# The moving operand of the big matmuls read as pairs of columns 256 apart

## The chip, the cores and the metric

The kernel runs on one core of one Trainium2 chip. A core has a matrix engine (TensorE, PE in the profile; its weight loads stand apart as PEld), VectorE (DVE), ScalarE (ACT), GpSimd (POOL) and SyncE (SP), which here issues nearly all DMA transfers. The metric is device time in microseconds, the median of several runs; work of the host before and after is not in it.

## The reference, cut to what matters

Attention over pooled keys and values, then a two-layer network with the activation h · erf(softplus(h)). All results are float32.

```python
k_p = k.reshape(B, H, S // 8, 8, D).mean(axis=3)      # B 8, H 8, S 576, D 64; v_p alike
attn = softmax(q @ k_p.T / sqrt(D))                   # 72 pooled keys
x = (attn @ v_p).transpose(0, 2, 1, 3).reshape(4608, 512)
h = x @ w_in                                          # 512 -> 2048
g = h * erf(log(1 + exp(h)))
out = g @ w_out                                       # 2048 -> 512
```

## The kernel before

**Layout.** Everything after the attention is kept transposed: features on the 128 partitions, tokens along the free dimension. The 4,608 tokens are cut into nine chunks of 512 (`TC`, `NC`). The stationary operand of a big matmul is a 128 x 128 block of a weight matrix, the moving operand a tile of 128 features by 512 tokens, and the result 128 features by 512 tokens in one bank of PSUM. A column of every moving tile, every bank and every output tile is thus one token.

**Three passes a product.** To come near float32, each operand is split into a high and a low part of type float32r (`halves`: a rounding copy on ScalarE or GpSimd, a subtraction on VectorE or GpSimd), and the helper `three` (line 817) issues three matmuls into the same bank: high x high, high x low, low x high. All big matmuls are on its line 821, as are the products of the later attention blocks with the split values (`att<-e,va` and `att<-e,vr` in the profile).

**Stages.** Chunk 0 runs plainly: `plain_in` computes its h, four feature tiles at a time, with the weights as they arrive and are split; `second` multiplies the activated tiles by w_out. The weights' parts are written to HBM tensors and read again later in pieces of 256 KB (`piece`). Chunks 1 to 8 run as four pairs s = 1 to 4. For each pair `quad` computes h by a scheme of seven products in place of eight (Strassen-Winograd: sums of weight blocks times differences of token tiles; `sides` makes the token tiles, `sums` the weight blocks). One call of the inner `product` (line 866) is six passes; a pair has 8 x 7 of them, 336 passes. The results are combined by VectorE (`t<-t,h`, `g<-t,h`), the activation runs on ScalarE (table loads, Softplus, Erf) and the multiplication by h on GpSimd or VectorE. The second layer of pair 1 goes through `second`; that of pairs 2 to 4 through `seconds`, again with seven products of 48 passes, whose moving operands are differences of g tiles (line 980), split anew. The last product of pair 4 goes through `rows`, output block by output block, its last pass cut into halves of 256 columns so that the end can be stored in pieces. The attention of the next tokens (`job`: scores in plain float32, transposes, values) is woven in between.

**What sets the order.** The program first lists operations, each with an engine, a cost in ns, a due time and the tiles that it reads and writes. `Program.once` (line 260) plays them as a list schedule over PE, ACT, DVE, POOL and SP: on each engine the operation that could start first, weighed against its due time, and within a window of due times; buffers and banks come from counted pools, and some operations may go to either of two engines. A DMA of 256 KB costs 720 ns on SP in this play, a float32r pass of 512 columns 227 ns on PE. `Program.order` (line 227) plays eight times; after each play it works out how late every operation could have ended (`latest`), and these times are the due times of the next. It keeps the due times that came out of the shortest play, shifts some of them, and emits the order of one more play. The shifts come from the tuple `MOVES`: each number in it seeds random offsets (of 300, 1,000 or 3,000 ns in spread) to the due times of all operations within 6, 20 or 60 us of one point. Each engine then executes its list in this order; waits are made from the tiles' uses. Fillers (small bf16 matmuls, line 1115) are put into PE's list where the play has it idle at the start.

The lines that matter for the change:

```python
at = list(best[1])                                   # due times left by the shortest play
for seed in MOVES:
    ...                                              # shifts part of `at`
for prios in ([t / UNIT for t in at], best[2]):
    ...
    return self.once()                               # the order that is emitted
```

Of the kernel before, what the change touches and what calls it, by code (L numbers as in the profile page):

```python
# [22 lines left out]
NP = H // 2  # L23
NT = B * S
DM, DF = 512, 2048
P = 128
TC = 512
NC = NT // TC
NJ = DF // P

# [10 lines left out]
BY_BLOCK = lambda ck: True  # L41
PASSES, UNIT = 8, 5100.0
SPREAD, REACH, SPAN = (300.0, 1000.0, 3000.0), (6e3, 20e3, 60e3), 860e3
MOVES = (
# [5 lines left out]
T0, T0_STEP = -10.5, 1.5  # L50
VAL_R = 3.5
KEYS, KEYS_R, KEYS_S = -5.5, 0.5, -1.0
# [37 lines left out]
def blocks():  # L90


    out, qo = [], 0
    for b in range(B):
        t = 0
        while t < S:
            ck, off = divmod(b * S + t, TC)
            n, tiles, fresh = min(256 if b < SPLIT else TC, S - t, TC - off), [], t == 0
            for at in range(0, n, P):
                T = min(P, n - at)  # L100
                tiles.append((qo, T))
                qo += P * NP * T
            out.append((ck, b, tiles, off, fresh))
            t += n
    return out


def mix(x):
# [273 lines left out]
def moe_attention(ctx: ExitStack, tc: tile.TileContext, cst, qa, kl, vl, wi, wo, out):  # L382
# [16 lines left out]
    op = pr.op  # L399
# [155 lines left out]
    xt, made, values_of = {}, {}, {}  # L555
# [261 lines left out]
    def three(o, w, x, first, last):  # L817

        (wh, wl), (xh, xl) = w, x
        for q, (u, v) in enumerate(((wh, xh), (wh, xl), (wl, xh))):  # L820
            nc.tensor.matmul(o, u, v, start=first and q == 0, stop=last and q == 2, skip_group_check=True)  # L821

    def activation(hs, prio):

        ys = [Buf(space, [P, 2, 512], F32, "d", "d") for _ in range(2)]
        y = lambda k: ys[k // 2].ap[:, k % 2]
        own = [(ys[k // 2], k % 2) for k in range(4)]

        for i in (0, 2):

            def softplus(i=i):
                for k in (i, i + 1):
                    nc.scalar.activation(y(k), hs[k][0].ap, AF.Softplus)  # L833

            op("ACT", 2 * act(512), prio + 0.01 * i, softplus, [h for h, _ in hs[i:i + 2]], own[i:i + 2], funcs="softplus")
        for k in range(2):
            op("ACT", act(1024), prio + 0.2, lambda k=k: nc.scalar.activation(ys[k].ap, ys[k].ap, AF.Erf),  # L837
               own[2 * k:2 * k + 2], own[2 * k:2 * k + 2], funcs="sigmoid")
        for k, (h, g) in enumerate(hs):
            if g is h:  # L840
                both(True, dve(512), gps(512), prio + 0.3, lambda e, k=k, h=h: e.tensor_mul(  # L841
                    h.ap, y(k), h.ap), [own[k], h], [h])
            else:
                op("DVE", dve(512), prio + 0.3, lambda k=k, h=h, g=g: nc.vector.tensor_mul(
                    g.ap, y(k), h.ap), [own[k], h], [g])

    def plain_in(ks, base):

        hs = []
        for k in ks:  # L850
            ft = order[k]
            hi, lo = load_in(ft, base + 0.5 * k)
            ph = bank("h")

            def gemm(ph=ph, hi=hi, lo=lo):
                for p in range(NP):
                    sl = slice(P * p, P * p + P)
                    three(ph.ap, (hi.ap[:, sl], lo.ap[:, sl]), [x.ap for x in xt[0][p]], p == 0, p == NP - 1)

            op("PE", 12 * 227, base + 0.5 * k, gemm, [hi, lo, *(x for q in xt[0] for x in q)], [ph])  # L860
            g = place("g")
            gs[0, ft] = g
            hs.append((ph, g))
        activation(hs, base + 0.5 * ks[-1] + 1)

    def product(o, w, name, x, prio, more, last):

        xs = [t for k in range(2) for t in x[name, k]]
        ws = [w] if isinstance(w, Buf) else w[:2]
        half = lambda l: w.ap[:, l] if isinstance(w, Buf) else w[l].ap[:, w[2]]  # L870

        def go():
            for k in range(2):
                sl = slice(P * k, P * k + P)
                three(o.ap, (half(0)[:, sl], half(1)[:, sl]), [t.ap for t in x[name, k]],
                      not more and k == 0, last and k == 1)

        op("PE", 6 * 227, prio, go, [*ws, *xs], [o], turn="p")

    def head(s, i, x, due):  # L880

# [68 lines left out]
    def second(ck, k, due, ws, part):  # L950

        g = gs[ck, order[k]]
        gh, gl = place("gl", F32R), place("gl", F32R)
        halves(lambda: g.ap, lambda: gh.ap, lambda: gl.ap, due - 1, [g], gh, gl, turn="g")
        if k == 0:
            po[ck] = [bank("o") for _ in range(NP)]
        for j0 in (0, 2):

            def gemm(j0=j0, o=po[ck]):
                for j in (j0, j0 + 1):  # L960
                    three(o[j].ap, [part(ws, j, l) for l in range(2)], (gh.ap, gl.ap), k == 0, k == NJ - 1)

            op("PE", 6 * 227, due + 0.12 * j0, gemm, [gh, gl, *ws], [po[ck][j0], po[ck][j0 + 1]])
        if k == NJ - 1:
            for j in range(NP):
                o, ot = po[ck][j], place("f")
                out_of_bank(512, due + 0.3, lambda ot=ot: ot.ap, lambda o=o: o.ap, [o], [ot])
                store(ck, j, ot, due + 0.4)

    def seconds(s, base, span):  # L970

        a, b = 2 * s - 1, 2 * s
# [9 lines left out]
        def product(n, weights, moving, combine, onto=None, last=True):  # L982
            o = onto or [bank("o") for _ in range(2)]
            for i in range(NQ):
                due = base + step * (n + i / NQ)
                if combine:
                    u, v = combine
                    less(moving[i], u[i], v[i], due - 1.2)
                g = moving[i]
                gh, gl = place("gl", F32R), place("gl", F32R)  # L990
                halves(lambda g=g: g.ap, lambda gh=gh: gh.ap, lambda gl=gl: gl.ap, due - 1, [g], gh, gl, turn="g")
                w = piece(*weights(i), due)

                def gemm(gh=gh, gl=gl, w=w, i=i):
                    for j in range(2):
                        sl = slice(P * j, P * j + P)
                        three(o[j].ap, (w.ap[:, 0, sl], w.ap[:, 1, sl]), (gh.ap, gl.ap),
                              onto is None and i == 0, last and i == NQ - 1)

                op("PE", 6 * 227, due, gemm, [gh, gl, w], o, turn="p")  # L1000
            return o, base + step * (n + 1)

        def add(dst, u, v, prio):
# [11 lines left out]
        def rows(n, weights, moving, add_to):  # L1015
            o = [bank("o") for _ in range(2)]
            ws, gs_ = [], []
            for i in range(NQ):
                due = base + step * (n + i / NQ / 2)
# [5 lines left out]
            for j in range(2):  # L1025
                for i in range(NQ):
                    due = base + step * (n + (i / NQ + j) / 2)
                    (gh, gl), w = gs_[i], ws[i]
                    end = i == NQ - 1
                    for u, m in ((0, 256), (256, 256)) if end and j else ((0, 512),):  # L1030
                        def gemm(j=j, i=i, gh=gh, gl=gl, w=w, cs=slice(u, u + m), end=end):
                            sl = slice(P * j, P * j + P)
                            three(o[j].ap[:, cs], (w.ap[:, 0, sl], w.ap[:, 1, sl]), (gh.ap[:, cs], gl.ap[:, cs]), i == 0, end)

                        op("PE", 3 * (m / 2.4 + 14), due, gemm, [gh, gl, w], [(o[j], u)] if m < 512 else [o[j]], turn="p")
                ot = place("f")
                for u, m in ((0, 256), (256, 256)) if j else ((0, 512),):
                    cs, key = slice(u, u + m), u if j else None
                    op("DVE", dve(m), due + 0.2, lambda ot=ot, j=j, cs=cs: nc.vector.tensor_add(  # L1039
                        ot.ap[:, cs], add_to[j].ap[:, cs], o[j].ap[:, cs]), [add_to[j], (o[j], key)], [(ot, key)])  # L1040
                    op("SP", 720 * m / 512, due + 0.3, lambda ot=ot, j=j, cs=cs: nc.sync.dma_start(
                        out[b, j][:, cs], ot.ap[:, cs]), [(ot, key)], [])
# [28 lines left out]
    gs, po = {}, {}  # L1071
# [89 lines left out]
```

## Time and profile before

| | us |
|---|---|
| median of 3 runs (lowest, highest) | 844.68 (844.62, 845.06) |
| span of the profiled execution | 844.4 |
| TensorE busy in it | 833.6 |
| VectorE, ScalarE, GpSimd busy | 676.7, 572.6, 448.2 |

The page of the profile gives the span, from the first to the last instruction, for the execution that was profiled; the other times come from runs without a profile. Busy time counts a stretch once even where two matmuls overlap in it. A TensorE instruction's mean duration includes the time until its result has landed, which the next instruction overlaps: for the pitch of a dense stretch its length is divided by the number of instructions. An idle time is put down to the engine or transfer whose signal came last.

### The profile page before, as it was taken

To read this page: it belongs to the slowest core of one execution; us is meant where nothing else is said; L and a number is where in the kernel's file an instruction comes from. 1 tells how busy PE (TensorE), PEld (TensorE's weight loads), DVE (VectorE), ACT (ScalarE), POOL (GpSimd) and SP (SyncE) were. 2 spreads that over 40 slices of the span, in tenths; PEclk is the share of its full clock that TensorE was granted. 3 is DMA by queue.
4 is the path that set the end of the run, shared out by engine and by line. 5 is a ranking of instruction groups with operands and counts; after the bars stand their busy time and mean duration, and the time that the engine had idled before them with its cause. 6 is when DMAs were issued, how large, how long until landed. Compare 5 with 4: busy or idle time off the path is not lost.

```text
span 844.4 us, 13334 instructions
## 1 busy us (share of the span) xinstructions
PE 833.6 (99%) x4042; PEld 692.6 (82%) x4042; DVE 676.7 (80%) x1238; ACT 572.6 (68%) x979; POOL 448.2 (53%) x437
## 2 busy tenths in 40 slices
PE   7999999999999999999999999999999999999998
PEld 6788888777888888888888888888888888888886
DVE  5977887857888897798998978878889866668872
ACT  5999976589965561779785643888857517776630
POOL 2996893676978740375774342657444503442310
PEclk9999999999999999999999999999999999999999
DMA  9999999999999799975575677934655778347641
GB/s 331 316 332 344 373 361 377 328 355 322 355 318 366 257 369 358 360 244 151 156 239 178 190 261 240 339 124 124 197 182 160 256 233 306 129 145 254 183 159 54
DMA packets 134695, 218.03 MB, mean 258 GB/s; under 512 B 17120, under 2 KB 49248, under 8 KB 134624
## 3 DMA queue, kind: packets, MB, share of 16 engines
q1 hardware_dynamic: 134624, 217.18, 75.3%
q8 instruction: 33, 0.54, 0.3%
q14 instruction: 38, 0.31, 0.1%
HBM read 167.84 MB, written 49.28 MB: 257 GB/s over the span
## 4 chain that ended last, share of the span: by engine, by line
PE 75%; DVE 1%; ACT 0%; DVEq 0%; issue 0%
PE o L821 37%; PE h L821 30%; PE att L632 3%; PE att L821 2%; PE att L687 1%; PE att L751 1%; PE att L690 0%; DVE g L841 0%; DVE gl L441 0%; PE att L750 0%; DVE e L703 0%; ACT e L701 0%; DVE f L1039 0%; DVEq L1157 0%
## 5 line engine op out<-in xcount | busy, mean ns | idle before, releaser
L821 PE MATMUL o<-gl,w 128*128 128x512 f32 x1536 | 359.3, 392 | 0.1
L821 PEld LDWEIGHTS o<-gl,w 128*128 128x128 f32 x1536 | 285.9, 188 | 60.0 <-DVE gl L441 0.5
L821 PE MATMUL h<-x,w 128*128 128x512 f32 x1344 | 312.6, 391 | 0.9 <-DVE t L917 0.7
L821 PEld LDWEIGHTS h<-x,w 128*128 128x128 f32 x1344 | 250.8, 188 | 54.4 <-DVE t L917 1.7
L841 POOL TENSOR_TENSOR g<-d,g 128x512 f32<-128x512 f32 x83 | 108.9, 1332 | 116.4 <-ACT d L837 116.4
L441 POOL TENSOR_TENSOR gl<-g,gl 128x512 fp32r<-128x512 f32 x64 | 98.7, 1551 | 77.7 <-ACT gl L429 64.9
L429 ACT ACTIVATE gl<-g 128x512 fp32r<-128x512 f32 x175 | 104.0, 625 | 45.4 <-PE o L821 20.4
L441 DVE TENSOR_TENSOR gl<-g,gl 128x512 fp32r<-128x512 f32 x144 | 103.4, 744 | 4.6 <-ACT gl L429 4.2
L917 DVE TENSOR_TENSOR g<-t,h 128x512 f32<-128x512 f32 x96 | 65.5, 684 | 28.0 <-PE h L821 26.0
L833 ACT ACT_TABLE_LOAD x49 | 62.9, 1283 | 20.7 <-PE h L821 20.0
L837 ACT ACTIVATE d<-d 128x1024 f32<-128x1024 f32 x72 | 74.1, 1056 | 0.5
L833 ACT ACTIVATE d<-g 128x512 f32<-128x512 f32 x103 | 59.6, 624 | 6.1 <-DVE g L917 5.6
L980 POOL TENSOR_TENSOR g<-g 128x512 f32<-128x512 f32 x34 | 47.2, 1387 | 27.5 <-DVE g L980 15.3
L917 DVE TENSOR_TENSOR t<-t,h 128x512 f32<-128x512 f32 x57 | 39.1, 686 | 22.6 <-PE h L821 19.8
L837 ACT ACT_TABLE_LOAD x44 | 56.5, 1283 | 0.8
L429 ACT ACTIVATE x<-xr 128x512 fp32r<-128x512 f32 (+2 forms) x53 | 28.9, 562 | 36.1 <-DVE xr L795 23.1
L632 PE MATMUL att<-kbd,q 128*128 128x144 f32 (+1 forms) x320 | 46.9, 288 | 0.1
L821 PE MATMUL h<-x,ws 128*128 128x512 f32 x192 | 46.0, 391 | 0.7 <-DVE g L917 0.7
L632 PEld LDWEIGHTS att<-kbd,q 128*128 128x128 f32 (+1 forms) x320 | 41.8, 179 | 4.4 <-issue 1.9
L980 DVE TENSOR_TENSOR g<-g 128x512 f32<-128x512 f32 x62 | 44.2, 721 | 0.7
L821 PEld LDWEIGHTS h<-x,ws 128*128 128x128 f32 x192 | 35.8, 188 | 8.8 <-DVE g L917 1.4
L641 DVE TENSOR_REDUCE m<-att 128x4 f32<-128x288 f32 (+1 forms) x80 | 34.5, 447 | 9.6 <-PE att L632 9.1
(105 smaller groups left out, 1089.5 us busy)
## 6 DMA issues: line engine op xcount, KB each, us to landing
w<-ws SPq DMA_DIRECT2D x192, 256.0 KB, 4.4
w<-wo SPq DMA_DIRECT2D x136, 256.0 KB, 4.2
w<-wi SPq DMA_DIRECT2D x96, 256.0 KB, 5.1
ws<-ws SPq DMA_DIRECT2D x64, 256.0 KB, 5.1
v<-vl SPq DMA_DIRECT2D x48, 256.0 KB, 5.1
out<-f SPq DMA_DIRECT2D x35, 256.0 KB, 2.1
k<-kl SPq DMA_DIRECT2D x32, 256.0 KB, 5.2
q<-qa SPq DMA_DIRECT2D x32, 256.0 KB, 5.1
```

The source lines that it names most:

```text
L429: op("ACT", act(n), prio, lambda: nc.scalar.activation(dst(), src(), AF.Copy, scale=scale), *access, turn=turn, alt=("POOL", 0.833 * n + 1 ...
L441: both(True, dve(n), gps(n), prio + 0.1, lambda e: e.tensor_sub(lo(), src(), f32(hi())), reads + [hikey], [lokey])
L632: nc.tensor.matmul(o, raw.ap[:, p, :T], kbd[:, p], start=(p % 2 == 0), stop=True, skip_group_check=True)
L641: op("DVE", dve(4 * SP), r + 0.4, lambda pv=pv, gs=gs: nc.vector.tensor_reduce(m.ap[:T, gs], pv(), AX.X, ALU.max), [ps], [(m, g)])
L687: nc.tensor.transpose(pa.ap[:, P * p:P * p + T], sp[:, p, 0:P], ident[:T, :T])
L751: nc.tensor.matmul(o[0:64], vb[0:96, p], etb.ap[0:96, p // 2, :n], start=False, stop=True, skip_group_check=True)
L821: nc.tensor.matmul(o, u, v, start=first and q == 0, stop=last and q == 2, skip_group_check=True)
L833: nc.scalar.activation(y(k), hs[k][0].ap, AF.Softplus)
L837: op("ACT", act(1024), prio + 0.2, lambda k=k: nc.scalar.activation(ys[k].ap, ys[k].ap, AF.Erf), own[2 * k:2 * k + 2], own[2 * k:2 * k + 2 ...
L841: both(True, dve(512), gps(512), prio + 0.3, lambda e, k=k, h=h: e.tensor_mul(h.ap, y(k), h.ap), [own[k], h], [h])
L917: op("DVE", dve(512), prio, lambda: nc.vector.tensor_add(dst.ap, u.ap, o.ap), [u, o], [dst])
L980: both(True, dve(512), gps(512), prio, lambda e: e.tensor_sub(out.ap, u.ap, v.ap), [u, v], [out])
```

## The change

A new helper `pairs` stands in place of `three` at the five places that issue big matmuls (`plain_in`, both `product`, `second`, `rows`). The moving tile is viewed as two halves of 256 columns, and the columns are read alternately from the two: 0, 256, 1, 257, and so on. The result is written into the bank in address order. So after each of the two layers the tokens of a chunk stand in another order; the order after both is `TOKEN`, and the host undoes it on the output. The products of the attention go on through `three`.

In the plan, the cost of a pass of 512 columns goes from 227 to 216.3 ns (`PASS`), that of a half pass of 256 columns from m / 2.4 + 14 to m / 2.4 + 3. The tuple `MOVES` is emptied.

```diff
+PASS = 216.3
...
-MOVES = (
-    31000001, 31000009, 31000022, 31000054, 31000055, 31000061, 31000085, 31000111, 31000112, 31000135, 31000169,
...
+MOVES = ()
...
+def pair_order(n):
+
+    j = np.arange(n)
+    return n // 2 * (j % 2) + j // 2
+
+
+TOKEN = pair_order(TC)[pair_order(TC)]
...
+    def pairs(o, w, x, first, last, cs=slice(0, TC)):
+
+
+        at = slice(cs.start // 2, cs.stop // 2)
+        three(o[:, cs].rearrange("p (a b) -> p a b", b=2), w,
+              [t.rearrange("p (b a) -> p a b", b=2)[:, at] for t in x], first, last)
...
-                    three(ph.ap, (hi.ap[:, sl], lo.ap[:, sl]), [x.ap for x in xt[0][p]], p == 0, p == NP - 1)
+                    pairs(ph.ap, (hi.ap[:, sl], lo.ap[:, sl]), [x.ap for x in xt[0][p]], p == 0, p == NP - 1)
-            op("PE", 12 * 227, base + 0.5 * k, gemm, [hi, lo, *(x for q in xt[0] for x in q)], [ph])
+            op("PE", 12 * PASS, base + 0.5 * k, gemm, [hi, lo, *(x for q in xt[0] for x in q)], [ph])
...
-                            three(o[j].ap[:, cs], (w.ap[:, 0, sl], w.ap[:, 1, sl]), (gh.ap[:, cs], gl.ap[:, cs]), i == 0, end)
+                            pairs(o[j].ap, (w.ap[:, 0, sl], w.ap[:, 1, sl]), (gh.ap, gl.ap), i == 0, end, cs)
-                        op("PE", 3 * (m / 2.4 + 14), due, gemm, [gh, gl, w], [(o[j], u)] if m < 512 else [o[j]], turn="p")
+                        op("PE", 3 * (m / 2.4 + 3), due, gemm, [gh, gl, w], [(o[j], u)] if m < 512 else [o[j]], turn="p")
...
-    return r.results[0]["out"].transpose(0, 3, 1, 2).reshape(NT, DM)
+    return r.results[0]["out"][..., np.argsort(TOKEN)].transpose(0, 3, 1, 2).reshape(NT, DM)
```

The other three places change in the same way as `plain_in`.

## Rows read from the trace of the kernel before

**Rows 1.** The page: span, busy time of the engines, TensorE's clock in 40 slices.

```profile
span 844.4 us, 13334 instructions
PE 833.6 (99%) x4042; PEld 692.6 (82%) x4042; DVE 676.7 (80%) x1238; ACT 572.6 (68%) x979; POOL 448.2 (53%) x437
PEclk9999999999999999999999999999999999999999
```

**Rows 2.** TensorE's waits, to 120 us, then after: us in total, times, longest.

```profile
PE att L1115 <- DMA cst<-cst: 2.7, 1, 2.7
PE att L690 <- POOL bb L675: 1.8, 2, 1.6
...
PE h L821 <- DVE g L917: 0.7, 1, 0.7
PE h L821 <- DVE t L917: 0.7, 1, 0.7
```

**Rows 3.** The chain that ended last: start us, length us, what.

```profile
688.46 76.16 PE h L821 x336
764.62 76.20 PE o L821 x339
```

**Rows 4.** Groups of the big passes: busy us, mean ns; then idle before.

```profile
L821 PE MATMUL o<-gl,w 128*128 128x512 f32 x1536 | 359.3, 392 | 0.1
L821 PE MATMUL h<-x,w 128*128 128x512 f32 x1344 | 312.6, 391 | 0.9 <-DVE t L917 0.7
L821 PEld LDWEIGHTS o<-gl,w 128*128 128x128 f32 x1536 | 285.9, 188 | 60.0 <-DVE gl L441 0.5 <-POOL w L441 0.4 <-issue 0.2
L821 PE MATMUL h<-x,ws 128*128 128x512 f32 x192 | 46.0, 391 | 0.7 <-DVE g L917 0.7
L821 PE MATMUL o<-gz,w 128*128 128x512 f32 x45 | 10.4, 389 | 0.0
```

**Rows 5.** Other matmuls: a chain piece, a group, three lines of the timeline.

```profile
240.77 1.96 PE att L632 x16
L1115 PE MATMUL att<-cst 128*128 128x256 bf16 x131 | 18.9, 300 | 2.7 <-DMA cst<-cst 2.7
23.54 1.58 PE L1115 MATMUL att<-cst 128*128 128x256 bf16 x13
294.33 0.40 PE L821 MATMUL att<-e,va 128*128 128x256 f32 x2
295.75 0.40 PE L821 MATMUL att<-e,va 128*128 128x256 f32 x2
```

**Rows 6.** Busy us by stretch, clock, DMA share, GB/s; last, L821 alone.

```profile
40.00:120.00 80.00, 79.89 (x391) 65.97 (x390) 66.22 (x120) 75.25 (x115) 67.43 (x77) 1.00 1.00 352
120.00:360.00 240.00, 238.37 (x1163) 199.14 (x1162) 195.12 (x369) 156.81 (x268) 145.75 (x146) 1.00 0.98 343
360.00:620.00 260.00, 259.91 (x1275) 216.85 (x1274) 225.01 (x432) 190.84 (x311) 149.87 (x138) 1.00 0.61 201
220.00:240.00 20.00, 20.00 (x95) 16.41 (x94) 17.03 (x32) 18.57 (x25) 18.12 (x17) 1.00 1.04 384
40.00:120.00 80.00, 68.68 (x294) 54.28 (x293) 1.00 1.00 352
120.00:360.00 240.00, 215.02 (x930) 171.25 (x929) 1.00 0.98 343
```

**Rows 7.** ScalarE and GpSimd: stepped and plain reads of 512 elements, mean ns.

```profile
L490 ACT ACTIVATE cv<-d 128x512 f32<-128x512 f32 x32 | 19.7, 625 | 2.0 <-DVE etb L719 1.1 <-ACT cv L490 0.4 <-DVE s L657 0.3
L429 ACT ACTIVATE gl<-g 128x512 fp32r<-128x512 f32 x175 | 104.0, 625 | 45.4 <-PE o L821 20.4 <-DVE g L980 17.5 <-DVE g L844 4.6
L496 POOL TENSOR_SCALAR low<-d 128x512 uint32<-128x512 uint8 x21 | 16.8, 798 | 20.7 <-DMA d<-wi 13.9 <-DMA d<-wo 5.6
L430 POOL TENSOR_SCALAR gl<-g 128x512 fp32r<-128x512 f32 x33 | 23.2, 706 | 18.6 <-PE h L821 7.4 <-PE o L821 7.3 <-DVE g L844 2.1
```

More of the change, by code (lines that the diff above doesn't have):

```diff
@@ L874, in go @@
                 sl = slice(P * k, P * k + P)
-                three(o.ap, (half(0)[:, sl], half(1)[:, sl]), [t.ap for t in x[name, k]],
+                pairs(o.ap, (half(0)[:, sl], half(1)[:, sl]), [t.ap for t in x[name, k]],
                       not more and k == 0, last and k == 1)
-        op("PE", 6 * 227, prio, go, [*ws, *xs], [o], turn="p")
+        op("PE", 6 * PASS, prio, go, [*ws, *xs], [o], turn="p")
     def head(s, i, x, due):
@@ L960, in gemm @@
                 for j in (j0, j0 + 1):
-                    three(o[j].ap, [part(ws, j, l) for l in range(2)], (gh.ap, gl.ap), k == 0, k == NJ - 1)
-            op("PE", 6 * 227, due + 0.12 * j0, gemm, [gh, gl, *ws], [po[ck][j0], po[ck][j0 + 1]])
+                    pairs(o[j].ap, [part(ws, j, l) for l in range(2)], (gh.ap, gl.ap), k == 0, k == NJ - 1)
+            op("PE", 6 * PASS, due + 0.12 * j0, gemm, [gh, gl, *ws], [po[ck][j0], po[ck][j0 + 1]])
         if k == NJ - 1:
@@ L996, in gemm @@
                         sl = slice(P * j, P * j + P)
-                        three(o[j].ap, (w.ap[:, 0, sl], w.ap[:, 1, sl]), (gh.ap, gl.ap),
+                        pairs(o[j].ap, (w.ap[:, 0, sl], w.ap[:, 1, sl]), (gh.ap, gl.ap),
                               onto is None and i == 0, last and i == NQ - 1)
-                op("PE", 6 * 227, due, gemm, [gh, gl, w], o, turn="p")
+                op("PE", 6 * PASS, due, gemm, [gh, gl, w], o, turn="p")
             return o, base + step * (n + 1)
```

4 rows, old and new, of the table MOVES are left out of this document.

## The prediction, made before the result was known

> **What bounds the kernel now.** The summary comes first: TensorE is busy 833.6 of 844.4 us, no other engine over 80%, and its clock is granted in full in every slice [rows 1]. As a busy TensorE is not one at its peak, the second view is who TensorE waits for. Hardly for anyone: the first constants, short waits while the attention starts up, and after 120 us two waits of 0.7 us each [rows 2]. The third view, the chain that ended last, is TensorE on TensorE for the last 152 us: 336 passes of 512 columns in 76.16 us, and 339 in 76.20, six of them half as wide [rows 3]. So the end is set by how many passes there are and by the time from one start to the next. That time is 76.16 / 336 = 226.7 ns. The mean of some 390 ns that the profile gives one pass [rows 4] holds its latency, which the next pass overlaps; the pitch is what counts.
>
> 512 columns at 2.4 GHz take 213.3 ns, so each pass pays 13.4 ns beyond its columns. Other forms pay less. The plain fp32 score matmuls run 16 records in 1.96 us, 122.5 ns each: for 144 columns that is twice 60.0 ns, and 2.5 over. The bf16 fillers take (1.58 - 0.30) / 12 = 106.7 ns for 256 columns, nothing over, with the group's mean of 300 ns taken for the last one's latency [rows 5]. The score matmuls take two cycles a column and the fillers read half as many bytes a column; only the float32r passes read four bytes at every cycle, and they do it in address order. So the 13.4 ns belong to this form, not to TensorE's issue as such, and the read pattern is the one part of the form that the change touches.
>
> **The change, part by part.**
>
> *The passes.* Full-width passes in the loops that the change touches: 1,536 + 1,344 + 192, and in the last product 45 and six halves, worth 48 [rows 4]: 3,120. (The 120 attention passes that go through the same helper keep their order.) Neither their number nor their weight loads change, and their output is written in address order as before. What one costs afterwards no row shows. From below: its columns alone, 213.3 ns, which takes 13.4 x 3,120 = 41.8 us off. From above: no row has TensorE with an alternating read, so the nearest are the other engines' stepped reads. ScalarE's read of one 4-byte word in eight bytes takes 625 ns, like its plain copy at 625; GpSimd's of one byte in eight takes 798 against 706 [rows 7], 13% more, by which a pass would take 256 ns and the kernel 3,120 x 29.5 = 92 us more. I take 213.3 + 2.5 = 215.8 ns, from the nearest row on the same engine with a four-byte operand: 10.9 x 3,120 = 34.0 us less. The weight loads, 188 ns at the mean [rows 4], still fit under that pitch.
>
> The Trainium skill (TensorE: Matmul & The Clock Gate, "Wait — 56ns, not 53.3ns?") gives a back-to-back matmul N / 2.4 GHz plus about 2.5 ns, 215.7 ns at 512 columns. The score matmuls here agree with it and the 226.7 ns of the big passes don't; with the page's figure the gain would be 11.0 x 3,120 = 34.3 us.
>
> *What is late next.* With 34 us less in TensorE, the stretches where something else is as full lose part of it. From 40 to 120 us the DMA engines are full (share 1.00, 352 GB/s) and ScalarE is busy 75.25 of 80; from 120 to 360 us the DMA share is 0.98 at 343 GB/s [rows 6]. At most 294 and 930 passes lie there, so TensorE would give 3.2 and 10.1 us, and the same bytes would have to come at 352 x 80 / 76.8 = 367 and 343 x 240 / 229.9 = 358 GB/s. If the present rates are the ceiling, all 13.3 us are lost; if the 384 GB/s of the best 20 us [rows 6] can be held, nothing. The wanted rates lie 47% and 37% of the way up, so I charge 1.5 + 3.7 = 5.2 us. After 360 us the DMA share is near 0.6, ScalarE 73% and DVE 87% of 260 us [rows 6]; a stretch 4.2% shorter leaves DVE at 90%, and I charge nothing, as TensorE there waits for nobody now. The wait that would come instead is a matmul's for a limb from DVE or GpSimd, and behind it the whole of TensorE's queue.
>
> *The order.* The list of 47 recorded moves goes, and every cost of a big pass in the plan falls from 227 to 216.3 ns; so the order on all five queues is a new one, SP's transfers among them. The order that is emitted is made from the due times that the best of eight passes leaves, and without moves nothing improves on it. What the moves were worth no row shows, since the trace has only the order with them. From below: the new order could take away the two waits after 120 us, 1.4 us. From above: every move had hidden one wait of 0.7 us like those [rows 2], 33 us. I take 8 us: the four paired stages have eight hand-overs (into each first product and into each second), at 1.0 us each, between the 0.7 and the 1.8 us of the waits that are left [rows 2].
>
> *The rest.* The host's reordering of the output is outside the device time; no store, load or elementwise operation changes its size, and the chain behind the last pass stays.
>
> **Sum**, against the profiled execution: 844.4 - 34.0 + 5.2 + 8 = 823.6 us. The median of the runs is 0.28 above that span; with it, 823.9.
>
> **The rivals.**
>
> *Others bind.* The passes get cheaper but the DMA engines keep their 13.3 us and the order costs 20 instead of 8: 844.7 - 34.0 + 13.3 + 20 = 844. For it: the first 360 us have no DMA share to spare, and ScalarE has 6% left from 40 to 120 us [rows 6]. Against it: over the whole span the bytes need only three quarters of the time, and after 360 us nothing is full. Its span is 834 to 846.
>
> *The pass keeps its time.* The 13.4 ns may not come from the read order. For it: attention passes of 256 columns, also float32r and in address order, take (295.75 - 294.33) / 12 = 118.3 ns, 11.7 over [rows 5]; so most of the surplus is per pass, not per column, as a start-up of this data type would be. Against it: a start-up can lie in the read, too. Then only the order changes: 844.7 + 8 = 852.7, from 843 to 878.
>
> *The pass gets dearer (the other side).* Each column would come from another place than the one before, 1 KB away, 512 times a pass and 3,120 passes. At GpSimd's 13% the time is 844.7 + 92 + 8 = 945 us. It decides from a pitch of 226.7 - 13.2 / 3,120 = 222.5 ns upwards, where the gain no longer pays for order and transfers; below it the surplus of 13.4 ns has to fall under 9.2. The ScalarE row speaks against it: a stepped read there costs nothing [rows 7]. The Trainium skill (SBUF — State Buffer, "Specifications (TRN2)") speaks for it: it gives SBUF lines of 16 bytes, wants at least two hits on a line for full bandwidth and lets each crossing to a new line cost something. By that rule the contiguous read has four hits in a row and the pair read none, and the change would slow every big pass. No row here shows TensorE crossing lines at each column; each line would still be used four times, only not in a row, so I leave the rule a small chance.
>
> **How the numbers follow.** Forecast (811 to 834 us): 0.60. Others bind: 0.22. The pass keeps its time: 0.10. Dearer: 0.08. The likeliest gives 824. The range runs from 811, which the gain of 34.0 us with hardly any loss gives (844.7 - 34.0 = 810.7), to 846, where "others bind" ends; outside lie most of the last two cases and a little below. About 0.2% (1.7 us) is what can be told from no change. Faster: 0.60, 0.20 of "others bind" and 0.01 of a better order alone, 0.81. Same: 0.02 + 0.02 = 0.04. Slower: what is left of the two last cases, 0.15.
>
> **What would show it.** The last product and the one before it are dense: 336 passes should take 336 x 215.8 = 72.5 us each instead of 76.2. If they take 76.2, the pass keeps its time; over 76.2, the line rule holds. TensorE's busy time should fall to about 800 us, and its idle time should rise from 10.8 to some 24, with waits on limbs (ScalarE, DVE, GpSimd) or on loaded weights, most of them before 360 us. If the idle time stays near 11, moves and transfers were charged too much and the time nears 811; if it passes 35, "others bind" holds. A DMA rate above 355 GB/s from 40 to 360 us would show that the transfers had room. The forecast is wrong if the pitch lies outside 214 to 219 ns, or if TensorE waits more than 25 us.

## The result, and the profile after

The changed kernel takes 836.49 us at the median (834.41 to 838.21) against 844.87 before (844.62 to 845.46): ratio 0.9901, 95% interval 0.9884 to 0.9918. It is faster by 8.4 us; 20.7 were forecast, and a range of 811 to 846. A run is 1.8 us longer than its span wherever both are known (836.5 the median, 835.4 the span of the profiled run, itself 837.19), before and after alike, so spans are compared with spans here. By this the profiled execution of the kernel before took some 846 us, and the 0.28 us that the prediction adds to its span sets different executions side by side; nothing below rests on it.

The page of the changed kernel, as [rows 1]:

```profile
span 835.4 us, 13512 instructions
PE 811.6 (97%) x4091; PEld 703.4 (84%) x4091; DVE 696.5 (83%) x1235; ACT 573.9 (69%) x976; POOL 445.2 (53%) x441
PEclk9998999999999999999999999999999999999999
```

TensorE lost 22.0 us of busy time, not the 34 of the forecast; VectorE, of whose work nothing was changed, gained 19.8. The last two products in the chain that ended last (start us, length us, what), as [rows 3]:

```profile
691.62 67.58 PE h L826 x312
759.20 72.61 PE o L826 x339
```

67.58 / 312 = 216.6 ns, and with its six half passes 72.61 / 336 = 216.1: the passes are as cheap as forecast. So the missing time is between them. TensorE's waits (us in total, times, longest), as [rows 2]:

```profile
PE o L826 <- DVE gl L446: 4.2, 3, 2.2
PE att L1127 <- DMA cst<-cst: 2.7, 1, 2.7
PE att L692 <- DVE g L856: 2.3, 1, 2.3
PE att L755 <- DVE f L503: 2.2, 2, 1.4
PE h L826 <- DVE t L929: 2.1, 1, 2.1
```

Behind the first constants it is now operands that VectorE makes. TensorE's idle time went from 844.4 - 833.6 = 10.8 to 835.4 - 811.6 = 23.8 us. And part of its busy time is no work. The fillers, of which there were 131 with 18.9 us [rows 5], are two groups now:

```profile
L1127 PE MATMUL att<-cst 128*128 128x256 bf16 x138 | 20.0, 302 | 2.7 <-DMA cst<-cst 2.7
L1127 PE MATMUL h<-cst 128*128 128x256 bf16 x42 | 5.3, 273 | 0.0
```

That is 6.4 us more; the second group, from 36 to 518 us, stands where the plan itself saw TensorE idle, and the kernel before had no such group. And after a wait the clock fell. Here is the timeline of TensorE around 65 us (start, length, what; in brackets the idle time before), then busy time and granted clock in stretches of 4 us (PE busy, clock, DMA share, GB/s):

```profile
65.73 0.43 PE L692 MATMUL att<-cst,s 64*128 64x64 f32 x4 [2.27 <-DVE g L856]
66.69 0.28 PE L695 MATMUL att<-cst,bb 64*64 64x64 f32 x1 [0.53 <-DVE g L856]
67.29 12.95 PE L826 MATMUL h<-x,w 128*128 128x512 f32 x45 [0.32 <-DVE g L856]
```

```profile
64.00:68.00 4.00, 1.42 (x7) 0.82 1.02 357
68.00:72.00 4.00, 4.00 (x11) 0.50 1.07 385
72.00:76.00 4.00, 4.00 (x17) 0.83 1.13 317
76.00:80.00 4.00, 4.00 (x20) 1.00 0.90 334
```

From 68 to 72 us TensorE ran at the lower level, 1.2 GHz: 11 matmuls fall into this stretch, 20 into the one from 76 to 80 us at the full clock. After a second long wait, 2.11 us until 233.82 us (`t` by VectorE), the clock fell again:

```profile
232.00:236.00 4.00, 2.18 (x5) 0.72 1.03 371
236.00:240.00 4.00, 4.00 (x19) 0.85 1.06 407
```

The mean clock of the whole execution is 0.993, against 1.000; 0.7% of 835.4 is 5.8 us, an upper estimate, as some of it lies where TensorE had nothing to do. Idle time (+13.0), fillers (+6.4) and clock (+5.8) add up to 25.2 us, and 34.0 - 25.2 = 8.8 is what the span fell by (9.0). By stretch, as [rows 6]:

```profile
40.00:120.00 80.00, 75.61 (x373) 64.15 (x372) 61.03 (x111) 75.02 (x108) 59.49 (x67) 0.96 0.95 326
120.00:360.00 240.00, 232.48 (x1180) 202.02 (x1179) 203.41 (x360) 154.99 (x264) 146.16 (x156) 0.99 0.95 334
360.00:620.00 260.00, 257.82 (x1318) 225.41 (x1317) 234.57 (x443) 188.27 (x311) 147.91 (x136) 1.00 0.66 219
```

The transfers, which were charged 5.2 us, run slower than before in the two stretches that were feared (326 and 334 GB/s, where 352 and 343 were moved), and their share went down to 0.95. So they were not full here.

### The profile page after: what moved, and what is told of

Same layout as the page of the kernel before. It is cut to its first block, busy times and chain, and to the rows that moved or that the text cites. A ratio compares the mean times of both kernels' runs of the same rounds, so it can differ in the third digit from the quotient of the medians.

```text
span 835.4 us, 13512 instructions
## 1 busy us (share of the span) xinstructions
PE 811.6 (97%) x4091; PEld 703.4 (84%) x4091; DVE 696.5 (83%) x1235; ACT 573.9 (69%) x976; POOL 445.2 (53%) x441
## 4 chain that ended last, share of the span: by engine, by line
PE 64%; DVE 6%; ACT 1%; issue 1%; DVEq 0%
PE o L826 31%; PE h L826 27%; PE att L637 3%; PE att L826 2%; PE att L692 1%; DVE s L684 1%; DVE gl L446 1%; PE att L756 1%; DVE e L708 1%; DVE vr L598 1%; DVE g L853 0%; DVE z L669 0%; ACT e L706 0%; DVE m L646 0%; ACT d L849 0%
## 5 line engine op out<-in xcount | busy, mean ns | idle before, releaser
L826 PE MATMUL o<-gl,w 128*128 128x512 f32 x1536 | 342.5, 381 | 4.7 <-DVE gl L446 4.2
L826 PE MATMUL h<-x,w 128*128 128x512 f32 x1344 | 302.8, 385 | 3.9 <-DVE t L929 2.1
L826 PEld LDWEIGHTS h<-x,w 128*128 128x128 f32 x1344 | 255.4, 192 | 43.4 <-DVE t L929 3.0
L853 POOL TENSOR_TENSOR g<-d,g 128x512 f32<-128x512 f32 x76 | 98.9, 1318 | 132.6 <-ACT d L849 85.0
L446 POOL TENSOR_TENSOR gl<-g,gl 128x512 fp32r<-128x512 f32 x63 | 90.7, 1445 | 77.9 <-ACT gl L434 73.4
L446 DVE TENSOR_TENSOR gl<-g,gl 128x512 fp32r<-128x512 f32 x145 | 114.3, 818 | 1.6 <-POOL gl L435 1.2
L992 POOL TENSOR_TENSOR g<-g 128x512 f32<-128x512 f32 x40 | 53.4, 1338 | 11.5 <-DVE g L992 5.1
L826 PE MATMUL h<-x,ws 128*128 128x512 f32 x192 | 44.1, 381 | 0.8 <-DVE x L446 0.5
```

The lines of the kernel that those rows point to most:

```text
L446: both(True, dve(n), gps(n), prio + 0.1, lambda e: e.tensor_sub(lo(), src(), f32(hi())), reads + [hikey], [lokey])
L992: both(True, dve(512), gps(512), prio, lambda e: e.tensor_sub(out.ap, u.ap, v.ap), [u, v], [out])
```

## The experiments

Two things had changed together, the read and the order, so the first four kernels part them. The theory was that the order ate the gain; the rival, that at the shorter pass some engine or the transfers are full whatever the order. The kernel before, timed anew beside each group of runs, took 844.35 to 845.60 us at the median; differences of about 1 us between the groups say nothing.

**e1, the pair reads in the order of before.** In the changed kernel:

```diff
-PASS = 216.3
+PASS = 227
-MOVES = ()
+MOVES = (31000001, 31000009, 31000022, ...)
-                        op("PE", 3 * (m / 2.4 + 3), due, gemm, ...
+                        op("PE", 3 * (m / 2.4 + 14), due, gemm, ...
```

> The pair reads alone: the order of the kernel before on all queues (its moves and its pass cost of 227 ns in the plan), and the big passes read as pairs. Order theory (the new order without moves is what ate the gain): the old order, made to hide everything at 226.7 ns a pass, keeps more of it at 215.9; TensorE waits under 15 us and the time is 815 to 826 us, clearly under that of the changed kernel. Rival (at the shorter pass some engine or the transfers are full, whatever the order): 832 to 838 us, as the changed kernel.

816.25 us, ratio 0.9668 (0.9652 to 0.9683). The rival falls. The page, the last two products, the waits, and the stretches from 40 to 120 and from 120 to 360 us:

```profile
span 816.5 us, 13382 instructions
PE 800.3 (98%) x4042; PEld 698.0 (85%) x4042; DVE 676.2 (83%) x1238; ACT 576.6 (71%) x979; POOL 453.2 (56%) x437
```

```profile
667.83 72.52 PE h L831 x336
740.35 72.56 PE o L831 x339
```

```profile
PE h L831 <- DVE g L934: 2.8, 3, 1.1
PE att L1132 <- DMA cst<-cst: 2.6, 1, 2.6
...
PE att L642 <- DMA q<-qa: 0.5, 1, 0.5
```

```profile
40.00:120.00 80.00, 77.66 (x386) 66.84 (x385) 64.49 (x119) 79.21 (x115) 69.44 (x75) 0.98 0.98 348
120.00:360.00 240.00, 235.09 (x1199) 205.71 (x1198) 203.45 (x382) 162.07 (x278) 150.38 (x152) 1.00 1.00 353
```

72.52 / 336 = 215.8 ns. TensorE is busy 800.3 us and idle 16.2. In the stretch from 40 to 120 us ScalarE (the fourth busy time) has 0.79 us left of 80, and the chain that ended last runs through it from 84 to 102 us. From 120 to 360 us the DMA engines have nothing left. TensorE's waits there are mostly for VectorE (`g<-t,h`, `t<-t,h`), but the chain behind three of them goes on to transfers:

```profile
169.77 4.09 DMA wo<-w
190.46 6.63 DMA k<-kl
216.42 6.84 DMA v<-vl
```

**e2, the moves alone.** In the kernel before:

```diff
-MOVES = (31000001, 31000009, 31000022, ...)
+MOVES = ()
```

> The kernel before with its list of moves emptied, nothing else: contiguous reads, 227 ns in the plan. Prediction's term: 8 us slower (853). If the moves were worth little at the old pass: 845 to 849 us, with a few us of waits for TensorE; then the loss in the changed kernel comes from the shorter pass under an order that nobody improved, not from the moves that were dropped as such.

850.21 us, ratio 1.0068 (1.0053 to 1.0083): 5.6 us above before, between the two expectations.

**e3, the new order with contiguous reads.** In the changed kernel (and the host's reordering with it):

```diff
-        three(o[:, cs].rearrange("p (a b) -> p a b", b=2), w,
-              [t.rearrange("p (b a) -> p a b", b=2)[:, at] for t in x], first, last)
+        three(o[:, cs], w, [t[:, cs] for t in x], first, last)
```

> The changed kernel with contiguous reads (its order, its plan's cost of 216.3 ns a pass, but the passes as before). Prices the pair read in the new order. If TensorE's waits in the changed kernel come from operands that are late because its passes got faster, slower passes let them catch up: TensorE waits and fillers shrink and the time is 846 to 855 us, 10 to 18 more than the changed kernel. If the waits are the order's own (fixed in place whatever the pass), all of 33.7 us come back: about 870 us.

863.00 us, ratio 1.0212 (1.0195 to 1.023). The order of the changed kernel costs 18.4 us even with the old passes, so most of the loss is in the order and not in the shorter pass. 26.5 of the 34 us come back, which lies between the two expectations. VectorE's extra work goes with the order too: it is busy 697.4 us here, with contiguous reads, and 676.2 in e1, with pairs in the old order.

**e4, new moves for the shorter pass**, 62 of them:

```diff
-MOVES = ()
+MOVES = (41000002, 41000003, 41000007, ...)
```

> The changed kernel with a list of 62 moves found for the shorter pass by playing the program's own plan; reads and costs as in the changed kernel. Order theory: 815 to 822 us, TensorE idle under 12 us. Rival (engines or transfers full): no order helps, 832 us or more, and TensorE's waits stay near 20 us.

827.11 us, ratio 0.9793 (0.9778 to 0.9807): neither. An order found for the shorter pass is 9.4 us better than the one without moves and still 10.9 behind the order of before.

**e5, the plan's old pass cost, no moves, pair reads.**

```diff
-PASS = 216.3
+PASS = 227
-                        op("PE", 3 * (m / 2.4 + 3), due, gemm, ...
+                        op("PE", 3 * (m / 2.4 + 14), due, gemm, ...
```

> The changed kernel with the plan's pass cost put back to 227 ns (and 14 in the half pass): pair reads, no moves. It splits the 20.2 us by which the changed kernel lies above the same reads in the old order. If the dropped moves are the loss: 836 us, as the changed kernel. If the moves are worth what they were at the old pass (5.6 us) and the rest comes from the order planned with the shorter pass: 820 to 824 us.

823.12 us, ratio 0.9739 (0.9719 to 0.9759), as the second branch has it. With e1 to e3 that fills a table (medians in us):

| order | contiguous | pairs 256 apart | worth of the pairs |
|---|---|---|---|
| 227 ns in the plan, moves | 844.6 | 816.25 | 28.3 |
| 227 ns, no moves | 850.2 | 823.1 | 27.1 |
| 216.3 ns, no moves | 863.0 | 836.5 | 26.5 |
| dropping the moves | 5.6 | 6.9 | |
| then the pass cost in the plan | 12.8 | 13.4 | |

The rows and columns nearly add. The reads are worth some 27 us in each of these three orders; the order costs 18 to 20, two thirds of it on the step to the new price of a pass in the plan.

**e6, without the fillers behind 36 us.**

```diff
-                if new and (start < FILL or idle > LONG_IDLE):
+                if new and start < 36000.0:
```

> The changed kernel without the 42 filler matmuls that the plan put into long idle stretches after 35.9 us; order and reads as they are. If the fillers stand in the way of work that is ready: up to 5.3 us (their busy time) faster, 831 to 835 us. If they only fill time in which TensorE would wait: the same, 835 to 838 us, with 5 us more of waits; more than that if the clock falls oftener.

835.39 us, ratio 0.9878 (0.9847 to 0.9908), within the scatter of the changed kernel. TensorE is busy 805.0 us and idle 28.9: the fillers stood in time that was lost anyway.

**e7 and e13, less work for VectorE.** The 88 pooling sums of k and v, first as copies of one key in eight, then as sums over one key:

```diff
-... nc.vector.tensor_reduce(to(), t.ap, AX.X, ALU.add)
+... nc.vector.tensor_copy(to(), <t.ap, element 0 of the eight>)              # e7
+... nc.vector.tensor_reduce(to(), <t.ap, element 0 of the eight>, AX.X, ALU.add)   # e13
```

> The changed kernel with the 88 pooling sums of k and v on VectorE replaced by copies of one key in eight (the attention then uses one key in eight; order, transfers and plan are as they are). It takes some 40 us of work from VectorE. If TensorE's waits in the changed kernel come from operands that are late because VectorE is behind: TensorE's idle and slow-clock time falls by 6 us or more, 822 to 830 us. If they are set by the order of TensorE's own queue or by transfers: within 3 us of the changed kernel.

> The changed kernel with the 88 pooling sums on VectorE cut to one key in eight, this time as sums of one element each in place of copies (the attention uses one key in eight; order, transfers and plan unchanged). Should take 40 to 50 us from VectorE. If VectorE's being behind makes TensorE wait: 820 to 830 us. If the waits are in the order itself: 833 to 837 us, as the changed kernel.

e7: 835.33 us (ratio 0.9885, 0.9865 to 0.9904), and it tells little: the copies took up to 1,326 ns and VectorE's busy time fell by 11.0 us only. In e13 a sum takes 260 ns in place of 675. Its page:

```profile
PE 809.3 (97%) x4091; PEld 701.7 (84%) x4091; DVE 666.4 (80%) x1235; ACT 574.4 (69%) x976; POOL 446.2 (54%) x441
```

30.1 us less for VectorE, and 832.58 us (ratio 0.9851, 0.9829 to 0.9872): 3.9 us for 30, between the two expectations and next to the second. VectorE's load is a small part of the loss; most of the waits for its operands do not come from it.

**e14, VectorE cheaper in the plan.**

```diff
-        return 1.15 * (n + 66) / 0.96
+        return 1.04 * (n + 66) / 0.96
```

> The changed kernel with one price in the plan changed: VectorE's operations at 1.04 in place of 1.15 times their cycle count (626 in place of 692 ns for 512 columns, where the trace shows 685 without a collision). No moves, pass cost 216.3, pair reads. If the plan at the shorter pass is bound by its price for VectorE and GpSimd, and pays with TensorE's order: 816 to 826 us, near the order planned with 227 ns (823). If the shorter pass cost spoils the order in another way: 832 to 838 us.

833.06 us (ratio 0.9855, 0.9834 to 0.9875). The second expectation holds: this price alone does not bring the order back. It also moved work: VectorE is busy 713.0 us in this run, GpSimd 392.4 in place of 445.2.

**e17 and e18, other pass costs in the plan**, no moves, pair reads:

```diff
-PASS = 216.3
+PASS = 222      # e17;  235 in e18
```

> The changed kernel (pairs 256 apart, no moves) with 222 ns in the plan for a pass (and 9 in the half pass), between the 216.3 of the changed kernel (836) and 227 (823). If the loss follows the plan's cost: 827 to 832 us. If orders scatter: anywhere from 820 to 840, outside that range as likely as in it.

> The same with 235 ns in the plan (22 in the half pass). If a plan that believes in a slower pass keeps more room: 817 to 823 us, not dearer than with 227. If orders scatter: anywhere from 818 to 840 us.

832.71 (ratio 0.9864, 0.9848 to 0.9880) and 828.12 us (0.9807, 0.9793 to 0.9822). With 216.3, 222, 227 and 235 ns in the plan the same reads take 836, 833, 823 and 828 us: not in step with the cost. Both runs miss the range of the theory that goes by the cost (827 to 832, 817 to 823) and lie in the range of scatter, which was so wide that it could hardly be missed. That orders scatter by ten microseconds fits all four, a trend up to 227 only three. So the 13 us of the table belong to two particular orders; how much of them is the cost and how much the chance of one order, four orders don't tell.

**e8 to e12 and e15, what in the read makes the pass cheap.** All in the order of before; only the order of the columns changes, here for pairs 4 apart and for a step of 2, with the result's view and the host's reordering (not shown) to match:

```diff
-              [t.rearrange("p (b a) -> p a b", b=2)[:, at] for t in x], first, last)
+              [t.rearrange("p (c b a) -> p c a b", b=2, a=4)[:, at] for t in x], first, last)   # e10
+              [t.rearrange("p (a b) -> p b a", b=2)[:, at] for t in x], first, last)            # e12
```

> Old order, moving operand described with the same three-dimensional pattern (256 groups of two) but the two columns of a pair adjacent, so that the addresses are in order as before the change. If the distance of the reads makes the pass cheaper: 226.7 ns a pass, 336 passes in 76.2 us, 844 us. If the form of the pattern does it: 216 ns, 72.6 us, 816 us.

> Old order, pairs of columns 2 apart within groups of four (0, 2, 1, 3): successive reads 4 or 8 bytes apart within 16 bytes. By the pitch of the 336 passes of the last first-layer product: if the gain needs reads from places far apart, 226.7 ns (76.2 us); if any departure from address order brings it, 216 ns (72.6 us).

> Old order, pairs 4 columns (16 bytes) apart within groups of eight. If neighbouring 16-byte pieces are far enough: 216 ns a pass (72.6 us for 336). If the distance has to be larger: 220 to 227 ns (74 to 76.2 us).

> Old order, pairs 16 columns (64 bytes) apart within groups of 32. If any reads from two places do: 216 ns a pass (72.6 us for 336). If the gain grows with the distance: between the pass at 4 columns apart and that at 256.

> Old order, even columns first, then odd ones: a plain step of 8 bytes, no alternation, each 16-byte piece read twice in a row and once more later. If alternation is what helps: 226.7 ns a pass or more (76.2 us for 336; a dearer one if crossing a 16-byte line every second column costs). If it is enough that successive columns are not adjacent: 216 ns (72.6 us).

> Old order, columns 0, 4, 8, ... first, then 1, 5, 9, ... and so on: a plain step of 16 bytes, each read from another 16-byte piece than the one before, without alternation. If it is the change of the 16-byte piece at every column that makes a pass cheap: 216 ns a pass, 336 in 72.6 us. If a piece has to be read again soon after (as the pairs do): as with a step of 2 or dearer, 453 to 907 ns a pass, 152 to 305 us for 336.

The 336 passes of the last first-layer product in the chain of each, for pairs 2 apart, pairs 4 apart (timed again as e16), a step of 2 and a step of 4:

```profile
687.90 76.16 PE h L831 x336
```

```profile
662.45 72.52 PE h L831 x336
```

```profile
1233.45 152.32 PE h L831 x336
```

```profile
1256.64 155.01 PE h L831 x336
```

| columns read | ns a pass | us |
|---|---|---|
| 0, 1, 2, 3 (e8: 76.16 us for 336) | 226.7 | 844.8 |
| 0, 2, 1, 3 (e9) | 226.7 | 845.7 |
| 0, 4, 1, 5 (e10) | 215.8 | 811.8 |
| 0, 16, 1, 17 (e11: 72.52 us for 336) | 215.8 | 813.7 |
| 0, 256, 1, 257 (e1) | 215.8 | 816.25 |
| 0, 2, 4, 6 (e12) | 453.3 | 1543.5 |
| 0, 4, 8, 12 (e15) | 461.3 | 1572.1 |

Pairs 8 bytes apart leave the pass as it was, pairs 16 bytes apart make it cheap (12 was not tried), and 64 bytes or 1 KB change nothing more in the pass. It isn't the form of the pattern (e8), nor leaving address order as such (e9). And a plain step, without the way back, doubles the pass; the clock is not behind that, its mean was 0.999 and 1.000 in e12 and e15. e8's ratio is 0.9999 (0.9989 to 1.0009); e9 to e12 and e15 were executed once each.

**e16, pairs 4 apart, timed.**

> Old order, pairs 4 columns apart, timed against the kernel before. If the 4 us of the single look are real: 810 to 813 us, ratio 0.960 to 0.963. If they were scatter: 815 to 818 us, as the pairs 256 apart in the same order.

813.34 us, ratio 0.9628 (0.9614 to 0.9643), below e1's interval: 2.9 us faster than pairs 256 apart in the same order, at the same pitch. The profiles differ in ScalarE and GpSimd. Here are ScalarE's reads of every second word and GpSimd's of one byte in eight in the weights' conversion, in e1, then ScalarE's in e16:

```profile
L500 ACT ACTIVATE cv<-d 128x512 f32<-128x512 f32 x32 | 24.3, 775 | 0.0
L506 POOL TENSOR_SCALAR low<-d 128x512 uint32<-128x512 uint8 x21 | 20.1, 959 | 18.4 <-DMA d<-wi 14.1 <-DVE f L508 2.0 <-DMA d<-wo 1.0
```

```profile
L500 ACT ACTIVATE cv<-d 128x512 f32<-128x512 f32 x32 | 19.8, 629 | 2.2 <-DVE etb L729 1.1 <-ACT cv L500 0.9
```

775 against 629 ns for ScalarE (625 before, [rows 7]), 959 against 788 for GpSimd (798 before, [rows 7]). With ScalarE's own byte reads (879 against 752) that is 24.3 + 9.7 - 19.8 - 8.3 = 5.9 us of ScalarE. ScalarE's word read takes 748 to 800 ns in all ten kernels with pairs 256 apart, and 625 to 635 in the eight with contiguous reads or pairs 1, 2, 4 or 16 apart; so it is the distance that slows it, in the same order of operations (e1 against e9 to e11). The two stretches in e16:

```profile
40.00:120.00 80.00, 78.90 (x401) 68.09 (x400) 66.95 (x123) 74.91 (x116) 68.31 (x78) 1.00 1.00 361
120.00:360.00 240.00, 236.83 (x1211) 207.87 (x1210) 204.45 (x387) 165.50 (x281) 149.26 (x153) 1.00 1.00 353
```

ScalarE has 5.09 us left from 40 to 120 us, where e1 had 0.79, and TensorE is busy 1.24 us more and at the full clock. That this is where the 2.9 us come from is likely and not shown: TensorE also gains 1.74 us from 120 to 360 us. This is the fastest kernel of the study.

## Why the prediction was wrong

*The passes: right.* 215.8 ns were taken, 215.8 measured, from the score matmuls' surplus over their columns. With the reads alone the gain would have been inside the range, and the two rivals on the pass itself (it keeps its time, it gets dearer) are refuted for this read. That the figure was met to a tenth is partly luck: it was taken over from another form of matmul, and no step said why reads from two places should cost less. Leaving address order is not enough for it (e9, e12).

*What is late next: right in size, right in half of its place.* 5.2 us were charged. In the order of before the reads brought 28.3 of 34.0, so 5.7 were lost. From 120 to 360 us, where 3.7 were charged to transfers, TensorE's idle time grew from 1.6 us [rows 6] to 4.9 in e1, with the DMA share at 1.00 and transfers in the chain behind its waits; they came at 353 GB/s, and 358 had been asked for. The sign that the text had set for room in the transfers, above 355 GB/s from 40 to 360 us, was not met (348 and 353). From 40 to 120 us, where 1.5 were charged to transfers, the idle time grew from 0.1 to 2.3 us and the clock was 0.98. There ScalarE was full, 79.21 of 80 us, partly because the pair read slowed its stepped reads. With pairs 4 apart, which leave them alone, only 3.0 us are lost (844.35 - 34.0 to 813.34). That a read of TensorE could make other engines slower was in none of the steps.

*The order: the step that failed.* The text took "8 us: the four paired stages have eight hand-overs"; 20.2 were measured (836.5 against 816.25), and these 12.2 us more are nearly all of the 12.6 by which 823.9 was missed. It priced the moves, and there it was near: 6.9. It named the other half, "every cost of a big pass in the plan falls from 227 to 216.3 ns; so the order on all five queues is a new one", and gave it no price. That half is 13.4 us in this order. The idle time of TensorE came out as forecast (23.8 for "some 24"), which looks like a hit and is none: the new order also brought 6.4 us of fillers and 5.8 us of slow clock, both of which count as busy. The forecast of 800 us of busy time is where that showed (811.6).

*The rivals.* The time lies in the range of "others bind", 834 to 846, but half of that mechanism didn't hold: the order cost the 20 us that it names, the transfers took at most some 3 of the 13.3 in the old order (e1) and were not full in the new one. On the Trainium skill's rule (SBUF — State Buffer, "Specifications (TRN2)"), two hits on a 16-byte line for full bandwidth and a cost for each crossing: pairs 4 apart cross at every column and make the pass cheaper, 215.8 ns, while a step of 2 has two hits in a row on each line and takes 453.3. The measurement decides against the rule for both. It fits the step of 4 (461.3), but the step of 2 is as dear.

*What stays open.* Why the order planned with the truer pass cost is 13 us dearer, and whether that is more than the chance of one order (e17, e18). VectorE's load gives 3.9 us of it back (e13), its price in the plan 3.4 (e14), the fillers 1.1 (e6, within the scatter); moves made for it give 9.4 of the whole 20.2 (e4). Why the pairs make a pass cheaper, the plain steps double it, and the distance of 1 KB slows ScalarE and GpSimd, was measured and not explained.

## What to carry to other kernels

Measure a change in the machine's work and a change in the order apart, by running each alone: here one gave 28 us and the other took 20, and the sum hid both. A new price in a planner is a new order, and is to be charged as one, even where the price is truer: without moves, the three other costs tried here gave orders 5 to 13 us dearer than 227 ns did. Count fillers and slow-clock time as lost time, as the busy share of an engine doesn't show either.

## What the runs showed of the hardware

- A float32r pass of 512 columns takes 226.7 ns in address order, 215.8 with columns read alternately from two places 16 bytes or more apart, and 453 to 461 with a plain step of 2 or 4 columns.
- With the two places 1 KB apart ScalarE's reads of one word in eight bytes take 775 ns and GpSimd's of one byte in eight 959 (e1); with 16 bytes apart they take 629 and 788 (e16), as beside reads in address order (625 and 798).
- After TensorE waited 2.27 us and 0.5 and 0.3 more, its clock was granted at half for the stretch from 68 to 72 us, though it was then busy throughout; after a wait of 2.11 us it was 0.72 from 232 to 236 us (the changed kernel).
